# Two linear-attention blocks on one core: the column sums of pk finished on VectorE through DRAM instead of on TensorE, with two rows of M loaded earlier

## The chip, the core and the metric

One of the eight cores of a Trainium2 chip runs the whole program. The metric is the time of one execution on the device in microseconds (us). Three runs of the kernel before took 577.52, 580.03 and 580.3 us, median 580.03.

The engines are named as in the profile: PE is TensorE (matmuls), DVE is VectorE, ACT is ScalarE, POOL is GpSimd, SP is SyncE, which here only issues DMAs. Each engine runs its own list of instructions in program order, and waits where a semaphore says that its operand is not there or its buffer not free.

## What is computed

Two independent blocks A and B, each with x of 2048 x 640, 32 heads of 20 columns, and fp32 throughout. The outputs of the two are laid side by side.

```python
qkv = (x @ wqkv).reshape(B, S, 3, H, Dh)...
phi = lambda t: jnp.where(t > 0, t + 1, jnp.exp(t)) + 1e-6
pq, pk = phi(q), phi(k)
kv  = jnp.einsum("bhsd,bhse->bhde", pk, v)
z   = jnp.einsum("bhsd->bhd", pk)
num = jnp.einsum("bhqd,bhde->bhqe", pq, kv)
den = jnp.einsum("bhqd,bhd->bhq", pq, z)[..., None] + 1e-6
return (num / den) ... @ wo
```

z, the column sums of pk over the 2048 rows, is what this change is about.

## The kernel before

Every fp32 product is made of three matmuls on halves: ACT rounds an operand to a high part (names that end in h), DVE subtracts it and keeps the low part (names that end in l: pkl, xnl, wql, xql, dsl), and PE adds high by high, high by low and low by high in PSUM (L209 to L211, and L349 for the products that save a multiplication by sums of quarters of the operands).

**The first phase** runs over the 32 tiles of 128 rows of x, block 0 (A) first and then block 1. Steps are PE's work, and jobs are the work of the other engines and the DMAs. Each step has a position; each job has a place beside a step. The tables MOVED (steps) and SHIFT (jobs) move them by hand-set numbers, and perform() (L397) issues all in the sorted order. That order, and nothing else, sets each engine's list.

- The steps ("p", i, n) are the products pk = x Wk of a pair of tiles (kprod, L494). ACT copies the results out of PSUM, DVE adds them (L356), ACT makes exp and relu, DVE mixes the two to ek (L564), POOL accumulates ek into a 128x640 tile in DRAM with an adding DMA (phi_z, L572, tile zd), ACT rounds to pkh (L576) and DVE makes pkl (L580).
- The steps ("G", i, s) and ("H", i, s, h) are the sums of x transposed times pk over four tiles (gsum, psg). DVE adds them to gacc (gacc_add, L650).
- After block 0 come kv = Wv x gacc, masked to the heads (kvmm, L776), and M = kv Wo (mev), stored to DRAM (md). Later rows of M are read back (load_w with "m", L233, tile wst), and DVE makes sums of them (form_sums1 and form_sums2, L854 to L862), which the products of the second phase need.
- Block 0's z: when all 16 tiles are in zd, SP reads the tile back (load_z, L731, tile zs), and five fp32 products with a column of ones (zmm, L733 to L737) make z in PSUM, five columns of 128. Each shows as two matmuls of 128x1 in the trace. z_out (L742 to L744) adds the epsilon on DVE and makes the sum of z.

**The second phase** has eight q groups u of 512 rows, four for each block. Its slots are written by hand: ("q", u, c, k) is product k of column block c of q = x Wq (psq), ("o", u, s) is stage s of the output product. at(slot, f, ...) hangs other work onto a slot, and run(slot) issues it there. In a group, ACT and DVE make phi of q (L944 to L946), DVE accumulates the denominators with z (qacc, L956), PE adds them over the heads (denmm, L967), DVE takes the reciprocal (L972), divides, and makes sums and splits of the quotient, and PE multiplies by the forms of M (outmm).

Block 1's kv and M are made inside the first q groups (kv_step, m_step). Block 1's zs is read back by SP just behind the loads of the first q group's x (xqs, xql), once the last accumulation into zd has landed. z_step, hung on ("q", 0, 1, 0), makes the ten matmuls and z_out. Block 1's z is first needed in group u = 4.

Between the phases stands a stretch in which DVE adds the last gsums (gacc of group 7), splits Wq (wql) and x (xql), while PE runs the last G and H steps, turns a part of gacc (T), and then starts ("q", 0, 0, 0). SP's loads of x for it (xqs, L277) wait for buffers that these splits free.

Of the kernel before, what the change touches and what calls it, by code (L numbers as in the profile page):

```python
# [14 lines left out]
H = 32  # L15
# [4 lines left out]
    ('c0', 10): 1.48, ('c0', 14): 1.59, ('c0', 3): 0.53, ('c0', 7): 1.14, ('c0', 8): 0.83, ('c0', 9): 2.95, ('c2',  # L20
    14): 0.45, ('c2', 6): 0.21, ('c2', 8): 1.01, ('c2', 9): 0.64, ('c4', 15): 0.47, ('c5', 10): 0.45, ('c5', 8):
    1.14, ('constants',): 2.19, ('exp', 0): 1.25, ('exp', 10): 0.43, ('exp', 11): 0.65, ('exp', 12): 2.78, ('exp',
    14): 0.41, ('exp', 15): 0.95, ('exp', 16): 0.91, ('exp', 2): 1.22, ('exp', 20): 0.06, ('exp', 22): 2.23, ('exp',
    23): 0.68, ('exp', 24): 0.16, ('exp', 25): 1.33, ('exp', 26): -0.21, ('exp', 28): 1.07, ('exp', 3): 4.78,
# [15 lines left out]
    2.01, ('gacc', 3, 3): 2.94, ('gacc', 4, 4): 0.78, ('gacc', 4, 5): 1.22, ('gacc', 7, 1): 0.62, ('gacc', 7, 2):  # L40
    1.9, ('kt', 1): 1.13, ('kvh', 4): 1.1, ('kvl', 0): 1.72, ('kvl', 1): 3.28, ('kvl', 2): 0.84, ('kvl', 3): 2.08,
    ('kvl', 4): 2.85, ('kvl', 5): 0.1, ('ld', 'k', 1, 1): -0.66, ('ld', 'k', 1, 2): 1.83, ('ld', 'k', 1, 3): -3.06,
    ('ld', 'k', 1, 4): 1.19, ('ld', 'm', 0, 0): 1.3, ('ld', 'm', 0, 2): 1.3, ('ld', 'm', 0, 4): 0.78, ('mix', 0):
# [1527 lines left out]
```

## Time and profile before

| | us |
|---|---|
| median of three runs | 580.03 |
| lowest, highest run | 577.52, 580.3 |
| the profiled execution | 580.78 |
| its span, first to last instruction | 579.0 |
| PE busy | 568.6 |
| DVE, ACT, POOL busy | 436.1, 335.8, 84.8 |
| mean granted PE clock | 0.996 |

How to read the rows that are quoted below. A row of the timeline begins with its start and its length in us, then the engine, the line, the operation, the tiles written and read (out<-in), the shape, and how many instructions were joined; in brackets stands the idle time before it and what ended it. PE's matmuls overlap, so the distance from one start to the next is what each one costs, not its length. A row of a group by line gives the total, the mean in ns, and the idle time before. A row of the waits gives total us, the number of waits, and the longest. In a table of windows the five pairs are the busy us (and instructions) of PE, PE's weight loads, DVE, ACT and POOL, then come the granted clock, the DMA share and GB/s.

### The profile page before, as it was taken

Reading aid. Unit: us, or ns where it says so; the run is one execution under the profiler, and the core shown is the slowest. Engines: PE = TensorE matmul, PEld = TensorE weight load, DVE = VectorE, ACT = ScalarE, POOL = GpSimd, SP = SyncE. Lnnn points to the kernel's source line nnn. Section 1 sums busy time; section 2 is a strip of 40 time slices with the busy share of each in tenths; the row PEclk is TensorE's granted clock in tenths of the full one; section 3 lists DMA queues with packets and bytes.
Section 4 is the critical chain, followed back from the end, with each engine's and each line's share of the span. In section 5 each row is a group of like instructions: output and inputs, shape, how many; then the busy total and the mean of one; then the engine's idle time right before and its main releaser. Section 6 shows DMA issues by size and latency. Waiting matters only on the chain.

```text
span 579.0 us, 9075 instructions
## 1 busy us (share of the span) xinstructions
PE 568.6 (98%) x3263; PEld 516.7 (89%) x3263; DVE 436.1 (75%) x724; ACT 335.8 (58%) x625; POOL 84.8 (15%) x141
## 2 busy tenths in 40 slices
PE   8999999999999999999989999999999999999997
PEld 6989999888999998978878889898998989898997
DVE  5889599877484868779735698977799776767792
ACT  5864567663674874746634865755657364545541
POOL 0111132411011211223200101311011200001010
PEclk9999999999999999999999999999999999999999
DMA  7968789899986877978989985764263994122022
GB/s 253 245 157 210 191 227 328 230 337 353 315 220 158 210 174 167 324 221 239 292 246 311 294 282 176 258 202 150 75 248 133 374 380 144 70 65 92 0 92 91
DMA packets 70260, 123.54 MB, mean 213 GB/s; under 512 B 7560, under 2 KB 32520, under 8 KB 70216
## 3 DMA queue, kind: packets, MB, share of 16 engines
q1 hardware_dynamic: 57912, 83.25, 44.9%
q0 software_dynamic: 12160, 39.66, 24.7%
q8 instruction: 25, 0.41, 0.3%
q14 instruction: 19, 0.16, 0.1%
q10 hardware_dynamic: 144, 0.07, 0.0%
HBM read 73.60 MB, written 49.35 MB: 212 GB/s over the span
## 4 chain that ended last, share of the span: by engine, by line
PE 86%; DMA 8%; DVE 2%; issue 2%; ACT 1%; SPq 1%; POOL 0%; DVEq 0%; POOLq 0%
PE pa L349 19%; PE pe L349 10%; PE psq L209 8%; PE psq L211 8%; PE psq L210 8%; PE psg L210 6%; PE psg L211 6%; PE psg L209 6%; PE psb L349 6%; PE psk L605 4%; DMA zd<-ek 3%; DMA wst<-md 2%; PE pskv L776 2%; DMA xn<-in_B_x 1%; DMA x<-in_A_xt_tiles 1%
## 5 line engine op out<-in xcount | busy, mean ns | idle before, releaser
L209 PE MATMUL psq<-xqh,wqh 128*128 128x512 f32 x200 | 79.2, 396 | 0.0
L210 PE MATMUL psq<-xql,wqh 128*128 128x512 f32 x200 | 78.5, 393 | 0.0
L211 PE MATMUL psq<-xqh,wql 128*128 128x512 f32 x200 | 78.4, 392 | 0.0
L210 PE MATMUL psg<-pkl,xnh 128*128 128x512 f32 x160 | 62.9, 393 | 1.4 <-DVE pkl L580 1.4
L209 PE MATMUL psg<-pkh,xnh 128*128 128x512 f32 x160 | 62.9, 393 | 0.0
L211 PE MATMUL psg<-pkh,xnl 128*128 128x512 f32 x160 | 62.5, 391 | 0.3 <-DVE xnl L199 0.3
L353 ACT ACTIVATE o<-pa 128x320 f32<-128x320 f32 x64 | 27.9, 438 | 45.2 <-PE pa L349 45.1
L946 DVE SCALAR_TENSOR_TENSOR pq<-eq,rq 128x512 f32<-128x512 f32 x40 | 27.6, 690 | 28.3 <-ACT rq L945 28.3
L572 POOL DMA_DIRECT2D zd<-ek x30 | 26.4, 881 | 133.1 <-DVE ek L564 65.2
L211 PEld LDWEIGHTS psq<-xqh,wql 128*128 128x128 f32 x200 | 38.0, 190 | 8.0
L210 PEld LDWEIGHTS psq<-xql,wqh 128*128 128x128 f32 x200 | 38.0, 190 | 7.4
L209 PEld LDWEIGHTS psq<-xqh,wqh 128*128 128x128 f32 x200 | 38.0, 190 | 7.3
L944 ACT ACTIVATE eq<-psq 128x512 f32<-128x512 f32 x40 | 23.8, 596 | 34.3 <-PE psq L211 32.0
L353 ACT ACTIVATE ko<-pa 128x320 f32<-128x320 f32 x52 | 22.4, 433 | 33.3 <-PE pa L349 33.0
L210 PEld LDWEIGHTS psg<-pkl,xnh 128*128 128x128 f32 x160 | 30.1, 188 | 7.7 <-DVE pkl L580 2.6
L576 ACT ACTIVATE pkh<-ek,epst 128x640 fp32r<-128x640 f32 x32 | 26.3, 826 | 17.9 <-DVE ek L564 17.9
L211 PEld LDWEIGHTS psg<-pkh,xnl 128*128 128x128 f32 x160 | 30.0, 188 | 7.3 <-DVE xnl L199 0.9
L209 PEld LDWEIGHTS psg<-pkh,xnh 128*128 128x128 f32 x160 | 30.1, 188 | 5.1
L650 DVE TENSOR_TENSOR gacc<-psg,gacc 128x512 f32<-128x512 f32 (+2 forms) x42 | 26.4, 628 | 6.9 <-PE psg L211 6.7
L202 ACT ACTIVATE dah<-pq 128x1024 fp32r<-128x1024 f32 (+5 forms) x27 | 18.2, 708 | 20.4 <-DVE pq L978 20.4
L580 DVE SCALAR_TENSOR_TENSOR pkl<-ek,pkh 128x640 fp32r<-128x640 f32 x32 | 26.1, 819 | 4.9 <-ACT pkh L576 4.9
L440 ACT ACTIVATE ksh<-sx 128x512 fp32r<-128x512 f32 x26 | 16.3, 627 | 23.1 <-DVE sx L458 22.9
(208 smaller groups left out, 1697.6 us busy)
## 6 DMA issues: line engine op xcount, KB each, us to landing
zd<-ek POOLq DMA_DIRECT2D x32, 320.0 KB, 5.1
out<-o POOLq DMA_DIRECT2D x28, 320.0 KB, 3.6
xql<-xd SPq DMA_DIRECT2D x24, 256.0 KB, 4.3
xn<-in_A_x SPq DMA_DIRECT2D x16, 320.0 KB, 4.8
...
xqs<-in_A_xt SPq DMA_DIRECT2D x20, 256.0 KB, 5.9
xqs<-in_B_xt SPq DMA_DIRECT2D x20, 256.0 KB, 4.4
```

The costliest lines, as they stand in the source:

```text
L209: nc.tensor.matmul(o, whi, xhi, start=first, stop=False)
L210: nc.tensor.matmul(o, whi, xlo, start=False, stop=False)
L211: nc.tensor.matmul(o, wlo, xhi, start=False, stop=last)
L349: nc.tensor.matmul(o, x, y, start=start and m == r == 0, stop=m == len(terms) - 1 and r == 2, skip_group_check=True)
L353: nc.scalar.activation(x, y, AF.Copy)
L572: nc.gpsimd.dma_start(zacc[b], e, accum_op=OP.add)
L576: nc.scalar.activation(pk[n][0], ek[n], AF.Identity, bias=epst)
L580: nc.vector.scalar_tensor_tensor(lo, ek[n], EPS, f32(hi), op0=OP.add, op1=OP.subtract)
L605: nc.tensor.matmul(kps["c", n][h], plain_x(n, c)[i], plain_w(c)[j][:, h * HF:(h + 1) * HF], start=(c == 0 and i == j == 0), stop=(c == NC ...
L650: nc.vector.tensor_tensor(o, x, o, op=OP.add)
L944: nc.scalar.activation(e, ps, AF.Exp)
L946: nc.vector.scalar_tensor_tensor(pq[u][:, c, :], e, 1.0, r, op0=OP.min, op1=OP.add)
```

## The change

The column of ones and zmm go. Each block's z is finished in these steps instead: read zd back (load_z); transpose it in 32x32 blocks on DVE and sum each block's 32 columns, 640 values a partition to 20 (z_turn); store 128x20 to DRAM (z_store); read it back as 32x4x5 in four DMAs so that the parts of one column lie on one partition (z_back, pieces of five floats); add the four parts, the epsilon and the total on DVE (z_out, now four operations).

Block 0's steps are jobs of the first phase: load_z beside ("p", 11, 0), z_turn beside ("p", 12, 3), z_store at ("g", 5, 3), z_back beside ("p", 14, 1), z_out at the first sum of group 7. Block 1's go into the second q group (u = 1) and the third.

The loads of rows 1 and 3 of M (form_jobs "m") move from ("p", 13, 4) to ("g", 5, 6). A new table AT moves six calls of the second phase by one or two slots. Of SHIFT and MOVED most entries are new: many steps and jobs change place with a neighbour. store_m takes one more argument, which it does not use.

```diff
-    ('c0', 10): 1.48, ('c0', 14): 1.59, ('c0', 3): 0.53, ('c0', 7): 1.14, ('c0', 8): 0.83, ('c0', 9): 2.95, ('c2',
+    ('c0', 10): 1.48, ('c0', 11): 0.04, ('c0', 12): 1.46, ('c0', 14): 3.31, ('c0', 3): 1.17, ('c0', 6): 0.26, ('c0',
...
+AT = {
+    ('denmm', 1): 2, ('kv_step', 1, 4): 2, ('m_step', 1, 3): 1, ('recip', 1, 0): 1, ('split_acc', 1): 1, ('z_turn',
+    1): 2,
+}
...
     def at(slot, f, *a):
+        slot = line[line.index(slot) + AT.get((f.__name__,) + a, 0)]
         todo.setdefault(slot, []).append((f, a))
...
-    ones = base.tile([P, 1], F32)
...
     def load_z(b):
-        wst["z", b] = base.tile([P, D], F32, name="zs", tag=f"wo{'hl'[b]}", bufs=2)
-        nc.sync.dma_start(wst["z", b], zacc[b])
-
-    def zmm(b):
-        x = wst["z", b]
-        zps[b] = bank("psz", "small")
-        for c in range(NC):
-            nc.tensor.matmul(zps[b][:, c:c + 1], x[:, c * P:(c + 1) * P], ones, start=True, stop=True)
+        zt[b] = base.tile([P, D], F32, name="zs", tag=f"wo{'hl'[b]}", bufs=2)
+        nc.sync.dma_start(zt[b], zacc[b])
+
+    def z_turn(b):
+        t = base.tile([P, D], F32, name="zt", tag=f"wo{'lh'[b]}", bufs=2)
+        nc.vector.transpose(t, zt[b])
+        zt[b] = base.tile([P, 2, 4 * NC], F32, name="zr", tag="kvt", bufs=3)
+        nc.vector.tensor_reduce(zt[b][:, 0].rearrange("p (j c) -> p c j", j=4),
+                                t.rearrange("p (c j a) -> p c j a", c=NC, j=4), axis=mybir.AxisListType.X, op=OP.add)
+
+    def z_store(b):
+        zr[b] = dram.tile([4, 32, 4 * NC], F32, name=f"zr{b}")
+        nc.sync.dma_start(zr[b].rearrange("i b c -> (i b) c"), zt[b][:, 0])
+
+    def z_back(b):
+        for j in range(4):
+            nc.sync.dma_start(zt[b][32 * j:32 * (j + 1), 1].rearrange("b (i c) -> b i c", i=4),
+                              zr[b][:, :, NC * j:NC * (j + 1)].rearrange("i b c -> b i c"))
 
     def z_out(b):
...
-        nc.vector.tensor_scalar(z, zps[b][:, :NC], S * EPS, None, op0=OP.add)
+        nc.vector.tensor_reduce(z, zt[b][:, 1].rearrange("p (i c) -> p c i", i=4),
+                                axis=mybir.AxisListType.X, op=OP.add)
+        nc.vector.tensor_scalar(z, z, S * EPS, None, op0=OP.add)
...
-            step(("z",), zmm, 0, after=[("zl",)])
...
-    form_jobs("m", 0, ([("g", 5, 5), ("p", 13, 4), ("g", 5, 5), ("p", 13, 4), ("g", 6, 1)],
+    form_jobs("m", 0, ([("g", 5, 5), ("g", 5, 6), ("g", 5, 5), ("g", 5, 6), ("g", 6, 1)],
...
-    job(("zl",), ("p", 9, 2), load_z, 0, after=[("zs", n) for n in range(NT)])
-    job(("zo",), ("z",), z_out, 0, after=[("z",)])
-    job(("zl1",), ("g", LG, 7), load_z, 1, after=[("zs", n) for n in range(NT, NN)])
+    job(("zl",), ("p", 11, 0), load_z, 0, after=[("zs", n) for n in range(NT)])
+    job(("zt",), ("p", 12, 3), z_turn, 0, after=[("zl",)])
+    job(("zw",), ("g", 5, 3), z_store, 0, after=[("zt",)])
+    job(("zb",), ("p", 14, 1), z_back, 0, after=[("zw",)])
+    job(("zo",), ("g", LG, 0), z_out, 0, after=[("zb",)])
...
-    at(("q", 0, 1, 0), z_step, 1)
+    at(("q", 1, 2, 3), load_z, 1)
+    at(("q", 1, 3, 3), z_turn, 1)
+    at(("q", 1, 4, 2), z_store, 1)
+    at(("q", 2, 0, 0), z_back, 1)
+    at(("q", 2, 2, 0), z_out, 1)
```

Three places of the lists, before and after. Line numbers of the changed kernel are higher by 21 to 37 (L210 becomes L231, L580 becomes L605).

**TensorE in the second column block of the first q group.** psq is the q product, psz the column sums of block 1, pskv the kv product of block 1. Before:

```order
L210 MATMUL psq<-xql,wqh 128x512
L211 MATMUL psq<-xqh,wql 128x512
L737 MATMUL psz<-ones,zs 128x1 x5
L776 MATMUL pskv<-gacc,wv 120x120 x5
L209 MATMUL psq<-xqh,wqh 128x512
L210 MATMUL psq<-xql,wqh 128x512
```

After:

```order
L231 MATMUL psq<-xql,wqh 128x512
L232 MATMUL psq<-xqh,wql 128x512
L809 MATMUL pskv<-gacc,wv 120x120 x5
L230 MATMUL psq<-xqh,wqh 128x512
L231 MATMUL psq<-xql,wqh 128x512
```

The five column-sum products are gone, and the kv product follows the q product.

**VectorE in the first phase, around the pkl of tiles 26 and 27** (ek and ko belong to phi, wst is a row of M, t_ the sums made of it). Before:

```order
L564 SCALAR_TENSOR_TENSOR ek<-ek,ko 128x640
L356 TENSOR_TENSOR ko<-pe,ko 128x320
L854 TENSOR_TENSOR t_3029<-wst 128x320
L855 TENSOR_TENSOR wst<-wst 128x320
L580 SCALAR_TENSOR_TENSOR pkl<-ek,pkh 128x640 x2
L861 TENSOR_TENSOR t_3029<-wst 128x320
L862 TENSOR_TENSOR t_3060<-wst,t_3029 128x320
```

After:

```order
L220 TENSOR_TENSOR fsl<-t_2822,fsh 128x320
L887 TENSOR_TENSOR t_3011<-wst 128x320
L888 TENSOR_TENSOR wst<-wst 128x320
L381 TENSOR_TENSOR ko<-pe,ko 128x320
L589 SCALAR_TENSOR_TENSOR ek<-ek,ko 128x640
L894 TENSOR_TENSOR t_3011<-wst 128x320
L895 TENSOR_TENSOR t_3029<-wst,t_3011 128x320
L605 SCALAR_TENSOR_TENSOR pkl<-ek,pkh 128x640 x2
```

The four operations on wst and t_ now all stand ahead of the pkl, and the last ek behind the first two of them.

**SyncE's queue in the same stretch** holds the loads of M (wst<-md), those of x (xn, xt) and the stores of x's halves (xd). Before:

```order
L233 DMA wst<-md_2200 128x640 x2
L417 DMA xn<-in_B_x 128x640 x2
L270 DMA xd_2452<-kal 128x3x128
L272 DMA xd_2452<-kal 128x128
L417 DMA xt<-in_B_xt_tiles 128x640
L270 DMA xd_2686<-kal 128x3x128
L417 DMA xn<-in_B_x 128x640
L272 DMA xd_2686<-kal 128x128
L417 DMA xn<-in_B_x 128x640 x3
L417 DMA xt<-in_B_xt_tiles 128x640
L233 DMA wst<-md_2200 128x640 x3
```

After:

```order
L260 DMA wst<-md_2186 128x640 x3
L299 DMA xd_2406<-kal 128x128
L297 DMA xd_2406<-kal 128x3x128
L260 DMA wst<-md_2186 128x640
L442 DMA xn<-in_B_x 128x640 x2
L297 DMA xd_2656<-kal 128x3x128
L442 DMA xn<-in_B_x 128x640
L442 DMA xt<-in_B_xt_tiles 128x640
L442 DMA xn<-in_B_x 128x640
L442 DMA xt<-in_B_xt_tiles 128x640
L442 DMA xn<-in_B_x 128x640 x2
```

Rows 1 and 3 of M (in the second load row before) stood behind eight loads of x; now they stand ahead of them.

**VectorE between the phases** (gacc<-psg adds the last gsums, wql and xql split Wq and x, z and zs are block 0's z_out). Before:

```order
L580 SCALAR_TENSOR_TENSOR pkl<-ek,pkh 128x640
L650 TENSOR_TENSOR gacc<-psg,gacc 128x3x128
L199 TENSOR_TENSOR wql<-wst,wqh 128x640
L650 TENSOR_TENSOR gacc<-psg,gacc 128x512
L199 TENSOR_TENSOR wql<-wst,wqh 128x640
L650 TENSOR_TENSOR gacc<-psg,gacc 128x2x128
L199 TENSOR_TENSOR wql<-wst,wqh 128x640
L650 TENSOR_TENSOR gacc<-psg,gacc 128x512
L199 TENSOR_TENSOR wql<-wst,wqh 128x640
L199 TENSOR_TENSOR xql<-xqs,xqh 128x2x128
L650 TENSOR_TENSOR gacc<-psg,gacc 128x512
L199 TENSOR_TENSOR xql<-xqs,xqh 128x2x128
```

After:

```order
L605 SCALAR_TENSOR_TENSOR pkl<-ek,pkh 128x640
L220 TENSOR_TENSOR wql<-wst,wqh 128x640 x2
L777 TENSOR_REDUCE z<-zr 128x5
L779 TENSOR_SCALAR z<-z 128x5
L780 TENSOR_REDUCE zs<-z 128x1
L781 TENSOR_SCALAR zs<-zs 128x1
L675 TENSOR_TENSOR gacc<-psg,gacc 128x3x128
L675 TENSOR_TENSOR gacc<-psg,gacc 128x512 x3
L675 TENSOR_TENSOR gacc<-psg,gacc 128x2x128
L220 TENSOR_TENSOR xql<-xqs,xqh 128x2x128
L220 TENSOR_TENSOR wql<-wst,wqh 128x640
L220 TENSOR_TENSOR xql<-xqs,xqh 128x2x128
```

z_out of block 0 and a second wql now stand ahead of the first sum, the five sums follow each other, and the other splits come after them.

More of the change, by code (lines that the diff above doesn't have):

```diff
@@ L19 @@
 SHIFT = {
-    ('c0', 10): 1.48, ('c0', 14): 1.59, ('c0', 3): 0.53, ('c0', 7): 1.14, ('c0', 8): 0.83, ('c0', 9): 2.95, ('c2',
[L21 to L24, printed above, removed]
[6 rows of a table removed]
@@ L31 @@
-    ('fdl', 'm', 0, 1): 0.25, ('fdl', 'm', 0, 3): 0.24, ('fdl', 'm', 0, 4): -0.49, ('fdl', 'm', 0, 6): 0.19, ('fdl',
[8 rows of a table removed]
[L40 to L43, printed above, removed]
@@ L92 @@
-    ('wol', 5): 0.05, ('wq', 0): 0.26, ('wq', 3): 0.21, ('wq', 4): 0.82, ('wqh', 0): -0.07, ('wqh', 1): -0.75,
-    ('wqh', 2): -1.14, ('wqh', 3): -1.22, ('wqh', 4): -3.33, ('wql', 0): -0.07, ('wql', 1): 1.4, ('wql', 2): -0.14,
[28 rows of a table removed]
-    -1.62, ('xq', 4): -2.08, ('xqh', 0): -0.26, ('xqh', 1): 0.24, ('xqh', 2): 0.5, ('xqh', 3): -1.19, ('xqh', 4):
-    -3.5, ('xql', 0): 0.23, ('xql', 1): -0.7, ('xraw', 0): -4.48, ('xraw', 1): 0.25, ('xraw', 2): -0.5, ('xraw', 3):
[3 rows of a table removed]
[4 rows of a table added]
+    10): 0.04, ('exp', 11): 0.73, ('exp', 12): 2.92, ('exp', 13): 3.23, ('exp', 14): 0.41, ('exp', 15): 0.95,
@@ new lines @@
+    ('exp', 16): 0.91, ('exp', 17): 0.07, ('exp', 18): -0.02, ('exp', 2): 0.61, ('exp', 20): -0.96, ('exp', 22):
+    1.7, ('exp', 25): 0.96, ('exp', 28): 1.07, ('exp', 3): 4.78, ('exp', 4): 0.2, ('exp', 5): 3.19, ('exp', 6):
[3 rows of a table added]
+    ('fdh', 'k', 1, 6): 0.01, ('fdh', 'k', 1, 8): 4.09, ('fdh', 'm', 0, 0): 1.04, ('fdh', 'm', 0, 1): 1.71, ('fdh',
[3 rows of a table added]
+    ('fdl', 'm', 0, 0): -0.93, ('fdl', 'm', 0, 1): -0.43, ('fdl', 'm', 0, 2): 1.2, ('fdl', 'm', 0, 3): 0.76, ('fdl',
[8 rows of a table added]
+    ('gacc', 0, 0): 0.46, ('gacc', 0, 1): 3.2, ('gacc', 0, 3): 0.36, ('gacc', 0, 5): 1.67, ('gacc', 0, 6): 1.73,
@@ new lines @@
+    ('gacc', 1, 1): 0.04, ('gacc', 1, 3): 0.64, ('gacc', 1, 5): 1.74, ('gacc', 1, 6): 1.99, ('gacc', 2, 1): 2.89,
+    ('gacc', 2, 3): 0.28, ('gacc', 3, 0): 0.42, ('gacc', 3, 1): 2.82, ('gacc', 3, 2): 2.99, ('gacc', 3, 3): 3.83,
+    ('gacc', 3, 5): 2.14, ('gacc', 3, 6): 1.96, ('gacc', 4, 0): 0.75, ('gacc', 4, 4): 2.17, ('gacc', 4, 5): 5.31,
+    ('gacc', 5, 0): 0.6, ('gacc', 5, 3): 1.28, ('gacc', 5, 5): 0.51, ('gacc', 5, 6): 1.36, ('gacc', 6, 2): 0.82,
+    ('gacc', 6, 4): 0.59, ('gacc', 7, 0): 0.31, ('gacc', 7, 1): 0.04, ('gacc', 7, 2): 2.56, ('gacc', 7, 4): 0.07,
@@ new lines @@
+    ('gacc', 7, 5): 0.78, ('gacc', 7, 6): 2.69, ('iota', 0): 1.42, ('kt', 0): 0.53, ('kt', 1): 1.13, ('kt', 5):
+    3.35, ('kvh', 0): 1.2, ('kvh', 1): 5.05, ('kvh', 4): 1.1, ('kvl', 1): 2.02, ('kvl', 2): 0.84, ('kvl', 3): 2.08,
+    ('kvl', 5): 1.36, ('ld', 'k', 1, 0): 1.32, ('ld', 'k', 1, 1): -0.06, ('ld', 'k', 1, 2): -2.17, ('ld', 'k', 1,
+    3): -3.61, ('ld', 'k', 1, 4): -1.63, ('ld', 'm', 0, 0): 1.22, ('ld', 'm', 0, 1): 1.16, ('ld', 'm', 0, 2): 1.48,
+    ('ld', 'm', 0, 3): -0.03, ('mc', 4, 1): 0.69, ('mix', 0): -0.53, ('mix', 10): 0.15, ('mix', 11): 0.24, ('mix',
@@ new lines @@
+    12): 0.49, ('mix', 13): 7.61, ('mix', 14): 4.05, ('mix', 15): 0.17, ('mix', 19): 1.66, ('mix', 20): 0.31,
+    ('mix', 23): 0.53, ('mix', 24): -0.1, ('mix', 26): 0.21, ('mix', 29): 2.36, ('mix', 3): -0.55, ('mix', 30): 0.8,
+    ('mix', 4): 3.06, ('mix', 5): 7.59, ('mix', 7): 1.86, ('mix', 8): 3.89, ('mix', 9): 1.16, ('ms', 0): -0.08,
[23 rows of a table added]
+    10): 1.37, ('relu', 11): 0.09, ('relu', 13): 1.06, ('relu', 14): 1.59, ('relu', 17): 1.12, ('relu', 2): 0.27,
+    ('relu', 21): 4.79, ('relu', 25): 2.55, ('relu', 28): 1.48, ('relu', 29): 0.1, ('relu', 30): 3.49, ('relu', 5):
[15 rows of a table added]
@@ new lines @@
+    -0.23, ('turn', 0, 0): 0.01, ('turn', 1, 0): 1.68, ('turn', 1, 1): 7.33, ('unit', 1): -2.53, ('v', 0): -0.59,
[6 rows of a table added]
+    1.07, ('woh', 1): -0.68, ('woh', 4): -0.51, ('wol', 0): 0.5, ('wol', 3): 0.03, ('wol', 4): 0.03, ('wq', 0):
+    -1.7, ('wq', 1): -0.97, ('wq', 3): -3.63, ('wq', 4): 9.05, ('wqh', 0): -2.09, ('wqh', 1): -2.1, ('wqh', 2):
+    -0.81, ('wqh', 4): -1.58, ('wql', 0): 0.07, ('wql', 1): -0.07, ('wql', 2): 7.63, ('wql', 3): 2.02, ('wql', 4):
[23 rows of a table added]
+    0): 1.47, ('xq', 2): -6.23, ('xq', 3): -7.53, ('xqh', 0): 0.62, ('xqh', 1): 0.38, ('xqh', 2): 0.96, ('xqh', 3):
@@ L127 @@
+    -1.51, ('xqh', 4): -0.13, ('xql', 0): 0.88, ('xql', 1): 0.44, ('xraw', 0): -2.59, ('xraw', 1): -1.73, ('xraw',
[4 rows of a table added]
 }
 MOVED = {
[7 rows of a table removed]
[13 rows of a table added]
+}
+AT = {
+    ('denmm', 1): 2, ('kv_step', 1, 4): 2, ('m_step', 1, 3): 1, ('recip', 1, 0): 1, ('split_acc', 1): 1, ('z_turn',
+    1): 2,
 }
@@ L214, in tile_linear_attn_pair @@
     todo = {}
+    line = []
+    for u in range(NU + 1):
+        line += [("q", u, c, k) for c in range(NC) for k in range(NC)] * (u < NU)
+        line += [("o", u - 1, s) for s in range(14)] * (u > 0)
     def at(slot, f, *a):
+        slot = line[line.index(slot) + AT.get((f.__name__,) + a, 0)]
         todo.setdefault(slot, []).append((f, a))
@@ L308, in constants @@
     def constants():
-        nc.vector.memset(ones, 1.0)
         ij = base.tile([P, P], I32, name="ij", tag="kvt", bufs=3)
@@ L724, in group_places @@
                 place["g", i, s] = share(i, 0.1 * (s + 1) if s >= halves else 0.15 + 0.05 * (s + 1))
[L726 removed]
+    zz, zt, zr, md, wvt, wot, kvt, kvp, mps = {}, {}, {}, {}, {}, {}, {}, {}, {}
     written = []
     def load_z(b):
[L730 to L737 removed]
+        zt[b] = base.tile([P, D], F32, name="zs", tag=f"wo{'hl'[b]}", bufs=2)
[13 more added lines that the diff above has]
+                              zr[b][:, :, NC * j:NC * (j + 1)].rearrange("i b c -> b i c"))
     def z_out(b):
@@ L745, in z_out @@
         zz[b] = z, s
-    def z_step(b):
-        zmm(b)
-        z_out(b)
     def load_v(b, g):
@@ L841, in m_step, with store_m @@
             m_out(b, g, h)
-    def store_m(eng):
+    def store_m(eng, g):
         eng.dma_start(*written.pop(0))
@@ L1401, in tile_linear_attn_pair @@
             job(("mc", g, k), ("m", g), m_out, 0, g, k, after=[("m", g)] + [("mc", g, 0)] * k)
-        job(("ms", g), place["m", g] + 1, store_m, nc.gpsimd, after=[("mc", g, 1)])
-    form_jobs("m", 0, ([("g", 5, 5), ("p", 13, 4), ("g", 5, 5), ("p", 13, 4), ("g", 6, 1)],
+        job(("ms", g), place["m", g] + 1, store_m, nc.gpsimd, g, after=[("mc", g, 1)])
+    form_jobs("m", 0, ([("g", 5, 5), ("g", 5, 6), ("g", 5, 5), ("g", 5, 6), ("g", 6, 1)],
                        [("g", 5, 8), ("p", 14, 4)], [("g", 5, 9), h(6, 1)], ("g", 6, 4),
@@ L1438, in tile_linear_attn_pair @@
         at((("q", 0, 2, 4), ("q", 0, 3, 4), ("q", 1, 0, 1), ("q", 1, 0, 3), ("q", 1, 1, 4), ("q", 1, 2, 4))[g],
-           store_m, nc.gpsimd)
+           store_m, nc.gpsimd, g)
     def forms(w, b, places):
```

6 lines of the change are left out of this document (removed), and 196 rows, old and new, of tables (MOVED, SHIFT).

## The prediction

> **What bounds the kernel now.** I read the busy times first, then the page's list of what TensorE waited for.
>
> ```profile
> PE 568.6 (98%) x3263; PEld 516.7 (89%) x3263; DVE 436.1 (75%) x724; ACT 335.8 (58%) x625; POOL 84.8 (15%) x141
> ...
> PE psz L737 <- DMA zs<-zd: 1.7, 1, 1.7
> PE psg L210 <- DVE pkl L580: 1.4, 2, 1.2
> ...
> PE psg L211 <- DVE pkl L580: 0.2, 1, 0.2
> PE pe L349 <- DVE o L356: 0.2, 1, 0.2
> ```
>
> PE is busy in 568.6 of 579.0 us. So a change can only gain by taking work off PE, by removing one of its few waits, or by removing time at a low clock. The longest wait, 1.7 us, stands before the column sums (psz, L737). The timeline of PE there, and the table of windows that covers the end of it (its columns after the five engines are the granted clock, the DMA share and GB/s):
>
> ```profile
> 296.92 0.39 PE L210 MATMUL psq<-xql,wqh 128*128 128x512 f32 x1
> 297.15 0.40 PE L211 MATMUL psq<-xqh,wql 128*128 128x512 f32 x1
> 299.25 1.28 PE L737 MATMUL psz<-ones,zs 128*128 128x1 f32 x10 [1.71 <-DMA zs<-zd]
> 300.39 1.41 PE L776 MATMUL pskv<-gacc,wv 128*120 128x120 f32 x10
> 301.46 0.78 PE L209 MATMUL psq<-xqh,wqh 128*128 128x512 f32 x1
> 302.04 0.63 PE L210 MATMUL psq<-xql,wqh 128*128 128x512 f32 x1
> ...
> 304.94 0.39 PE L211 MATMUL psq<-xqh,wql 128*128 128x512 f32 x1
> 301.41:304.83 3.42, 3.42 (x11) 2.74 (x10) 1.09 (x3) 1.04 (x2) 0.00 (x0) 0.50 1.06 248
> ```
>
> Here three losses follow each other: 1.71 us of idling, 1.14 us of zmm (299.25 to 300.39), and 3.42 us with the clock granted at 0.50. The chain of waits says why the sums came late:
>
> ```profile
> 288.94 7.21 DMA zd<-ek
> 296.27 2.94 DMA zs<-zd
> ```
>
> The last accumulation into DRAM (zd) took 7.21 us, its reading back 2.94, and PE stood behind both.
>
> **What the change removes.** Block 0 has the same ten matmuls without a wait:
>
> ```profile
> 165.29 1.21 PE L737 MATMUL psz<-ones,zs 128*128 128x1 f32 x10
> 166.36 0.48 PE L209 MATMUL psg<-pkh,xnh 128*128 128x512 f32 x1
> ```
>
> The next matmul starts 1.07 us later. Both zmm leave PE for good: 1.07 + 1.14 = **2.21 us**. The wait on zs goes too: **1.71**. Nothing else is late there: the next step on PE, kv_step(1, 1), needs a weight load that the changed order issues earlier than before.
>
> The half clock: from 301.46 to 304.94 eight matmuls start. At full speed their starts are 0.23 us apart (296.92 and 297.15), so 8 x 0.23 = 1.84 instead of 3.48: **1.64 us**, if the gap ahead of them causes it. I take it so, because it is the only halved stretch between start and end and it follows directly on the longest stretch without wide matmuls (297.4 to 301.4).
>
> [...]
>
> The second wait sits at 249. On DVE (first three rows) and PE (the others):
>
> ```profile
> 248.80 0.49 DVE L854 TENSOR_TENSOR t<-wst 128x320 f32<-128x320 f32 x1 [2.22 <-DMA wst<-md]
> 249.32 0.49 DVE L855 TENSOR_TENSOR wst<-wst 128x320 f32<-128x320 f32 x1
> 249.74 1.55 DVE L580 SCALAR_TENSOR_TENSOR pkl<-ek,pkh 128x640 fp32r<-128x640 f32 x2
> ...
> 249.05 0.40 PE L209 MATMUL psg<-pkh,xnh 128*128 128x512 f32 x1
> 250.60 0.50 PE L210 MATMUL psg<-pkl,xnh 128*128 128x512 f32 x1 [1.16 <-DVE pkl L580]
> ```
>
> DVE idles 2.22 us for a row of M that was loaded behind loads of x, does two form sums, and only then makes the pkl that PE wants. In the changed order rows 1 and 3 of M are issued ahead of eight loads of x instead of behind them, so all four form sums stand ahead of that pkl with their data long there. The start distance on PE is 1.55 against 0.23, so 1.3 is to be had. The pkl now follows its own chain (ek, pkh on ACT) and ends at about 249.2 by my count, just when PE wants it. I take **1.2**.
>
> The short waits. A wait of 0.2 in the list costs more than its idle time, since the next start is late by the pipeline as well:
>
> ```profile
> 357.44 0.46 PE L349 MATMUL pe<-f,dah 128*128 128x320 f32 x2
> 357.73 0.31 PE L349 MATMUL pe<-f,dal 128*128 128x320 f32 x1
> 358.21 0.42 PE L349 MATMUL pe<-fh,dsh 128*128 128x320 f32 x1 [0.17 <-DVE o L356]
> ```
>
> Starts 0.48 apart where 0.15 is usual (two in the 0.29 from 357.44): 0.33 for a listed 0.17. Three such waits are touched: this one (a reciprocal on DVE stood ahead of o and is moved behind it), the second pkl wait of L210 (1.4 - 1.16 = 0.24 listed) and that of L211 (0.2), whose pkl are made earlier or used later. Twice the listed 0.6 is 1.2; I take **1.05**.
>
> Sum of the gains: 2.21 + 1.71 + 1.64 + 1.2 + 1.05 = **7.8 us**.
>
> **What it adds.** The trace of before has neither a transpose nor a reduction of 128x640 on DVE. The nearest rows are the cheapest and the dearest rate of DVE:
>
> ```profile
> L972 DVE RECIPROCAL rd<-psd 128x256 f32<-128x256 f32 x16 | 27.8, 1745 | 0.9 <-PE psd L967 0.9
> L580 DVE SCALAR_TENSOR_TENSOR pkl<-ek,pkh 128x640 fp32r<-128x640 f32 x32 | 26.1, 819 | 4.9 <-ACT pkh L576 4.9
> 208.00:215.20 7.20, 6.98 (x41) 6.11 (x39) 4.42 (x7) 5.90 (x10) 1.75 (x2) 1.00 0.60 125
> 346.67 1.22 DVE L199 TENSOR_TENSOR dsl<-sr,dsh 128x1024 fp32r<-128x1024 f32 x1
> 351.28 0.31 PE L349 MATMUL pa<-fh,dsh 128*128 128x320 f32 x1
> ```
>
> By L580 each costs 0.82, so a z_turn 1.6 us; by the reciprocal's rate (1.745 x 640/256 = 4.36) 8.7. All plain 128x640 rows of DVE lie at 0.82, so I take 1.6. [...]
>
> Block 0's turn stands at about 207. DVE is busy 4.42 of the 7.20 us after 208 (the fourth pair in the window row), so 2.8 us of slack hide it before the next pkl that PE waits for (the 0.24 of L210) is due. Block 1's turn stands in the second q group, where DVE runs behind PE, between two splits, ahead of the dsl that ends at 347.89; PE first uses that half of the sums at 351.28. Cover: 3.4 us. Both at nothing; without the cover it would be 1.6 each.
>
> The stores and loads of z (128x20, and 512 pieces of 20 bytes) run on SP's queue. Each has at least 10 us between issue and use; the smallest transfers of before landed in 2.9 to 5 us. Nothing.
>
> The place that does cost is the entry into the q phase. The last sums of block 1 on DVE, their first user on PE, and the loads of x that follow:
>
> ```profile
> 281.88 0.83 DVE L580 SCALAR_TENSOR_TENSOR pkl<-ek,pkh 128x640 fp32r<-128x640 f32 x1 [0.90 <-ACT pkh L576]
> L650 DVE TENSOR_TENSOR gacc<-psg,gacc 128x512 f32<-128x512 f32 (+2 forms) x42 | 26.4, 628 | 6.9 <-PE psg L211 6.7
> L199 DVE TENSOR_TENSOR wql<-wst,wqh 128x640 fp32r<-128x640 f32 x10 | 8.1, 811 | 0.3 <-ACT wqh L238 0.3
> L743 DVE TENSOR_REDUCE zs<-z x2: 157/158/158, 169.0 to 300.8; 128x1 f32<-128x5 f32 x2
> 286.17 0.39 PE L209 MATMUL psg<-pkh,xnh 128*128 128x512 f32 x1
> 288.36 0.42 DVE L199 TENSOR_TENSOR xql<-xqs,xqh 128x256 fp32r<-128x256 f32 x1
> 286.08 1.39 SPq L277 DMA_DIRECT2D xqs<-in_A_xt  x2
> xqs<-in_A_xt SPq DMA_DIRECT2D x20, 256.0 KB, 5.9
> 292.14 1.16 ACT L290 ACTIVATE xqh<-xqs 128x512 fp32r<-128x512 f32 x2 [0.39 <-DMA xqs<-in_A_xt]
> 293.55 0.39 PE L209 MATMUL psq<-xqh,wqh 128*128 128x512 f32 x1
> ```
>
> After the pkl (end 282.7) DVE now has two wql (2 x 0.8), the four small operations of z_out (4 x 0.16), and only then the sums gacc 5, 0, 2, 1, 6. That puts the second of them at 282.7 + 1.6 + 0.7 + 0.5 + 0.6 = 286.1. PE, freed of the L211 wait just ahead (0.4 by the doubling above), wants that bank at about 286.17 - 0.4 = 285.8: a wait of 0.3, or twice that if the fifth sum, which the turn of gacc on PE needs, is late too; I take **0.5**. Further, the last load of x (issued by 286.08 + 1.39 = 287.5 before) now waits for the xql that ends about 288.1. In before that load landed 4.7 us after its issue, at 292.1, and ACT made two xqh by 293.3, used at 293.55. Now: 288.1 + 4.7 to 5.9, plus 1.2 on ACT, is 294.0 to 295.2 against a use at 293.55 + 0.4 = 294.0: 0 to 1.2. I take **0.35**. What the refitted tables do elsewhere (over a hundred steps and jobs change place by one or two neighbours) I could follow only at the tightest places; for it I set down **0.4**, between nothing and rival (c).
>
> The sum: 7.8 - 0.5 - 0.35 - 0.4 = 6.55. The profiled execution took 580.78 (span 579.0), which gives 574.2; it lies 0.75 above the median of 580.03, which would give 573.5. I take **574.0**, nearer to the execution that the rows come from.
>
> **The rivals.** A measurement of this kernel can tell about 0.5% from no change, so "same" is 577.1 to 582.9.
>
> (a) A new wait takes the place of the old one at the q entry: the late load of x lands at 295.2 or later, PE waits 1.2 to 1.5 us amid narrow kv matmuls, and the clock halves again (1.64). Loss about 3.2 on the forecast: 577.2. For: ACT idled 0.39 us for this load in before already. Against: it is issued only 0.6 us later.
>
> (b) The halved stretch does not come from the gap and stays: 574.0 + 1.64 = 575.6. For: the gap of 1.16 us at 249 halved nothing, so a gap alone does not do it. Against: its place. [...]
>
> (c) The new order of the neighbours brings as many short waits as it takes: the 1.2 of pkl and the 1.05 come back elsewhere, and one more of 1.2 with them: 574.0 + 3.5 = 577.5. For: at 249 and 357 (rows above) PE waited for work that DVE merely had in an unlucky order. Against: I found no such place in the order.
>
> (d) Slower: DVE's transpose and reduction run at the reciprocal's rate. A turn of 8.7 us exceeds the cover by 8.7 - 2.8 = 5.9 in block 0 and 8.7 - 3.4 = 5.3 in block 1, both on PE: 574.0 + 11.2 = 585.2. It passes 582.9 once a turn takes more than 7.6 us (2 x 7.6 - 6.2 = 9.0). For: only that no row shows them. Against: the other 128x640 rows are all near 0.82.
>
> **How the numbers follow.** Forecast (571.2 to 576.5) 0.58; (a) 0.13; (b) 0.10; (c) 0.12; (d) 0.07. (a) and (c) lie just past 577.1; three tenths of their 0.25 count as faster: 0.58 + 0.10 + 0.07 = 0.75. The rest of them is same: 0.18; slower is (d): 0.07. Low end: all gains, no cost, from the median: 580.03 - 7.8 = 572.2, and 1 us for the spread of the runs (577.52 to 580.3): 571.2. High end: (a) or (c) with 1 us more: 578.7.
>
> **What would show it.** Right: no psz rows; the granted clock at 1.00 from start to end; PE's list without zs, with pkl at 249 gone or under 0.3; transpose and reduction near 0.8 us each; short waits at the q entry on gacc, on xqh or both. Wrong: a wait above 1 us at the first psq matmuls (a); a 0.50 stretch without a long gap ahead of it (b); new pkl, xnl or ko waits that sum to 3 us (c); a turn above 3 us with PE waiting on dsl (d).

## The result and the profile after

The changed kernel took 573.01 us (median of 7 runs, 571.96 to 575.27) against 577.61 (7 runs, 577.41 to 580.3): a ratio of 0.9917, 95% interval 0.9892 to 0.9943. Measured again beside the kernel before (a_repeat below), it was 573.51 against 579.45, ratio 0.9898 (0.9871 to 0.9925). The ratios come from the single runs and are not the quotients of the medians; the two differ by up to 0.2%. The forecast was 574.0, a gain of 6.0 to 6.55; the two measurements give 4.6 and 5.9. The profiled executions lie further apart: spans 579.0 and 571.0.

PE's busy time and its whole list of waits, after:

```profile
PE 564.1 (99%) x3243; PEld 514.1 (90%) x3243; DVE 438.2 (77%) x729; ACT 334.5 (59%) x625; POOL 84.5 (15%) x141
...
PE psq L230 <- ACT xqh L317: 1.2, 1, 1.2
PE psi L1124 <- DVE idle L1121: 1.0, 1, 1.0
PE pa L374 <- ACT ko L378: 0.5, 1, 0.5
PE psk L630 <- DVE wl L220: 0.4, 1, 0.4
PE pa L374 <- ACT mev L378: 0.2, 1, 0.2
```

No wait on zs, none on pkl, none on o; and 20 instructions fewer on PE. Two waits are new: xqh, 1.2 us, now the longest, and mev, 0.2 us. The timeline of PE at the place of the old column sums, and the table of windows over the q entry (the granted clock is the last column but two):

```profile
294.33 0.39 PE L232 MATMUL psq<-xqh,wql 128*128 128x512 f32 x1
294.56 1.21 PE L809 MATMUL pskv<-gacc,wv 128*120 128x120 f32 x10
...
285.00:290.00 5.00, 4.42 (x20) 3.28 (x18) 2.62 (x4) 0.59 (x2) 0.00 (x0) 1.00 0.93 287
290.00:295.00 5.00, 4.38 (x27) 3.85 (x28) 1.00 (x4) 2.80 (x7) 0.00 (x0) 1.00 0.80 240
```

The kv product follows the q product at the usual 0.23 us, at full clock. The two windows hold 1.2 us in which PE is not busy, and that is the xqh wait. How it comes about, on PE, DVE, SP and ACT in turn:

```profile
289.02 0.40 PE L232 MATMUL psq<-xqh,wql 128*128 128x512 f32 x1
290.62 0.50 PE L230 MATMUL psq<-xqh,wqh 128*128 128x512 f32 x1 [1.20 <-ACT xqh L317]
...
280.46 2.71 DVE L675 TENSOR_TENSOR gacc<-psg,gacc 128x384 f32<-128x384 f32 x5
283.08 0.41 DVE L220 TENSOR_TENSOR xql<-xqs,xqh 128x256 fp32r<-128x256 f32 x1
283.53 0.33 SPq L304 DMA_DIRECT2D xqs<-in_A_xt  x1
289.41 1.15 ACT L317 ACTIVATE xqh<-xqs 128x512 fp32r<-128x512 f32 x2 [7.09 <-DMA xqs<-in_A_xt]
```

Five sums of gacc run without a pause on DVE (280.46 to 283.17), then xql frees the buffer, SP issues the last load of x at 283.53, it lands 5.9 us later, and only then does ACT make the two xqh.

The two new operations of DVE, by line:

```profile
L760 DVE STREAM_TRANSPOSE zt<-zs 128x640 f32<-128x640 f32 x2 | 1.7, 837 | 0.0
L762 DVE TENSOR_REDUCE zr<-zt 128x20 f32<-128x640 f32 x2 | 1.6, 821 | 0.1
```

A turn costs 1.66 us, as the 128x640 rows had it.

### The profile page after: what moved, and what is told of

Same layout as the page of the kernel before. It is cut to its first block, busy times and chain, and to the rows that moved or that the text cites. A ratio compares the mean times of both kernels' runs of the same rounds, so it can differ in the third digit from the quotient of the medians.

```text
span 571.0 us, 9065 instructions
## 1 busy us (share of the span) xinstructions
PE 564.1 (99%) x3243; PEld 514.1 (90%) x3243; DVE 438.2 (77%) x729; ACT 334.5 (59%) x625; POOL 84.5 (15%) x141
## 4 chain that ended last, share of the span: by engine, by line
PE 87%; DMA 6%; ACT 3%; DVE 2%; issue 1%; SPq 0%; POOL 0%; DVEq 0%; ACTq 0%; POOLq 0%
PE pa L374 21%; PE pe L374 10%; PE psq L230 8%; PE psq L232 8%; PE psq L231 8%; PE psb L374 6%; PE psg L232 6%; PE psg L231 6%; PE psg L230 6%; PE psk L630 4%; PE pskv L809 2%; DMA md<-mev 2%; DMA zd<-ek 1%; DMA wst<-md 1%; DMA xqs<-in_A_xt 1%
## 5 line engine op out<-in xcount | busy, mean ns | idle before, releaser
L231 PE MATMUL psq<-xql,wqh 128*128 128x512 f32 x200 | 77.9, 389 | 0.0
L231 PE MATMUL psg<-pkl,xnh 128*128 128x512 f32 x160 | 62.7, 392 | 0.0
L231 PEld LDWEIGHTS psq<-xql,wqh 128*128 128x128 f32 x200 | 37.6, 188 | 7.2
L231 PEld LDWEIGHTS psg<-pkl,xnh 128*128 128x128 f32 x160 | 30.0, 188 | 5.7 <-DVE pkl L605 0.3
L220 DVE TENSOR_TENSOR xnl<-xn,xnh 128x640 fp32r<-128x640 f32 x32 | 25.9, 820 | 6.9 <-ACT xnh L509 6.8
L605 DVE SCALAR_TENSOR_TENSOR pkl<-ek,pkh 128x640 fp32r<-128x640 f32 x32 | 25.9, 821 | 6.5 <-ACT pkh L601 6.3
```

Of the source, the lines that this page charges most:

```text
L220: nc.vector.tensor_tensor(lo, src, f32(hi), op=OP.subtract)
L231: nc.tensor.matmul(o, whi, xlo, start=False, stop=False)
L605: nc.vector.scalar_tensor_tensor(lo, ek[n], EPS, f32(hi), op0=OP.add, op1=OP.subtract)
```

## The experiments

All medians stand beside runs of the kernel before on the same chip. Where less than one per cent matters the rows of the profiles are read first, since single times of one kernel scatter by 2 to 8 us.

**The kernel before once more (b_repeat).**

> The kernel before, unchanged. Its runs so far lie at 577.4 to 577.9 and at 580.0 to 580.8. Theory A: the difference is two things that fall out differently from run to run, the half-clock stretch behind the wait on zs (1.6 us) and PE's wait at the start on the first pieces of x (1.3 us). Then the wait on zs (1.7 us) is in this profile again, near 297 us, and the time follows the other two: about 577.5 with neither, 580.8 with both. Rival B: the half clock always follows the wait, and the runs differ elsewhere; then a 0.50 stretch of 3.4 us stands behind the wait in this profile too, whatever the time.

Measured: 579.79 (before beside it 579.53), span 578.3. On PE, and the windows around the wait and behind it:

```profile
298.58 1.27 PE L737 MATMUL psz<-ones,zs 128*128 128x1 f32 x10 [2.08 <-DMA zs<-zd]
...
296.10:300.14 4.04, 1.96 (x16) 1.56 (x15) 0.90 (x3) 1.64 (x3) 0.00 (x0) 1.00 0.91 270
300.15:303.56 3.41, 3.41 (x14) 2.99 (x13) 0.94 (x5) 1.04 (x2) 0.00 (x0) 0.50 1.03 277
```

The wait is there again, 2.08 us, and the clock halves again for 3.41 us. The 1.3 us at the start (PE on the first pieces of x) is not. The changed kernel's profile does not have it either, and the next PE row that both share starts 1.0 us earlier there (9.08 against 10.08). ACT waited 0.78 us for a piece of x there in the profile of before, and in that of the change not at all. So it was one execution's luck with a transfer, and about 1.0 of the 8.0 us between the two profiles has nothing to do with the change. The mean clock was recorded for 73 executions of this kernel, ten of this run and 63 beside the experiments. In 29 it is 0.999 to 1.000, mean time 578.0; in 30 it is 0.996 or 0.997 (one halved stretch of 3.41 in 577), mean 579.8; in 14 it is 0.993 or 0.994 (two; the profile of a_oldrows below has 6.82 us at half clock and 0.994), mean 581.5. So an execution takes about 1.8 us more for each stretch, and before had 0.79 of them on average (58 in 73). The changed kernel's 11 executions with a recorded clock all have 0.999 or 1.000. Theory A holds in its main point: both profiles have the wait, and the half clock comes in only a part of the executions. Against rival B speaks the next run, whose profile has a wait of 1.95 us at a clock of 0.999.

**Only the matmuls of block 1's sums later (b_late).**

```diff
-    at(("q", 0, 1, 0), z_step, 1)
+    at(("q", 0, 3, 0), z_step, 1)
```

> The kernel before with one edit: the ten column-sum matmuls of block 1 stand two column blocks later in the first q group, when their data has landed. zmm stays on PE (1.1 us), only the wait goes. Theory A: the wait of 1.7 us goes and with it any half clock, so 1.7 to 3.4 us less than before, 0.994 to 0.997 of it, with no row psz <- zs in PE's list of waits. Rival C (the gain needs PE to be rid of zmm, or the wait moves to what stands behind it on SP's queue, the weight loads of kv): under 1 us gained, and PE waits for a weight load near 297 instead.

Measured: ratio 1.0006 (0.9983 to 1.0029), 578.71. A miss. PE, DVE, ACT and SP:

```profile
303.86 1.31 PE L776 MATMUL pskv<-gacc,wv 128*120 128x120 f32 x10 [1.95 <-DVE kvt L783]
302.79 0.82 DVE L199 TENSOR_TENSOR wol<-wo,woh 120x640 fp32r<-120x640 f32 x1 [3.95 <-ACT woh L805]
302.02 0.74 ACT L805 ACTIVATE woh<-wo 120x640 fp32r<-120x640 f32 x1 [3.50 <-DMA wo<-in_B_wo]
...
287.28 3.26 SPq L754 DMA_DIRECT2D wv<-in_B_wv  x3
294.51 0.33 SPq L731 DMA_DIRECT2D zs<-zd  x1
294.93 1.33 SPq L754 DMA_DIRECT2D wv<-in_B_wv  x3
296.35 2.88 SPq L766 DMA_DIRECT2D wo<-in_B_wo  x6
```

The wait moved to a later kv step and kept its size. load_z(1) still stands in SP's queue, between two halves of the loads of wv, until the last accumulation has landed: SP is held from 290.54 to 294.51, 4.0 us. The loads of wo stand behind it; kvt stands behind wol on DVE, and PE behind kvt. Rival C had the queue right and named the wrong load.

**Load and matmuls both in the second q group, still on PE (b_free).**

```diff
-    job(("zl1",), ("g", LG, 7), load_z, 1, after=[("zs", n) for n in range(NT, NN)])
...
-    at(("q", 0, 1, 0), z_step, 1)
+    at(("q", 1, 2, 3), load_z, 1)
+    at(("q", 1, 4, 0), z_step, 1)
```

> The kernel before with block 1's column sums still on PE, but both the load of zs and the matmuls moved to the second q group, so that SP's queue is not held up in front of the loads of wo. With only the matmuls moved, PE waited 1.95 us for kvt behind a late wo instead. Theory A (what cost the time was the load of zs that blocks SP's queue, not zmm): neither wait is left between 290 and 310, the clock stays at 1.00, and the span is 1.7 to 3.4 us below that of before, 575 to 576.5. Rival G (the loads that now run together delay xqs or wv): a new wait above 0.7 us on xqh or pskv between 290 and 310, span 577 or more.

Measured: ratio 0.9945 (0.9915 to 0.9976), 575.56 against 579.45, span 573.2, clock 0.999 or 1.000 in all five runs. The top of PE's list, and SP's loads of wo:

```profile
PE psi L1091 <- DVE idle L1088: 1.0, 1, 1.0
PE pa L349 <- ACT ko L353: 0.5, 1, 0.5
...
293.78 2.87 SPq L766 DMA_DIRECT2D wo<-in_B_wo  x6
```

Nothing waits between 290 and 310 any more; wo is issued 2.6 us sooner than in b_late (296.35). Theory A, and the gain of 3.9 us is more than the 1.7 to 3.4 expected. About two thirds of the change's gain on the same chip (3.9 of 5.9) is had by moving block 1's load and matmuls, without VectorE. What is left to the changed kernel (573.51) is 2.05 us. That is near the 2.21 of zmm, but it is no measurement of zmm: the rows of M, the refitted tables and the new wait on xqh lie in the same difference.

**Only the rows of M earlier (b_rows).**

```diff
-    form_jobs("m", 0, ([("g", 5, 5), ("p", 13, 4), ("g", 5, 5), ("p", 13, 4), ("g", 6, 1)],
+    form_jobs("m", 0, ([("g", 5, 5), ("g", 5, 6), ("g", 5, 5), ("g", 5, 6), ("g", 6, 1)],
```

> The kernel before with one edit: the loads of rows 1 and 3 of M at the earlier place. Theory A: the pkl wait near 249 us (1.16 listed, 1.3 to 1.4 in start distances) goes and nothing takes its place: 1.2 to 1.4 us less, 0.998 of before. Rival D: the x loads that now stand behind them come later and PE waits for xnl or ko in the same stage: no change, with a new wait of 0.5 to 1.5 us between 235 and 270.

Measured: ratio 0.9978 (0.9952 to 1.0004), 578.34: the time does not tell the two apart. The profile shows both: the pkl wait at 249 is gone, and a wait of 0.7 on ko near 236 has come (in the second line of its list; the other 0.5 was there before).

```profile
PE psz L737 <- DMA zs<-zd: 1.3, 1, 1.3
PE pa L349 <- ACT ko L353: 1.2, 2, 0.7
```

And the wait that was to be saved varies from one execution to the next: 1.16 at this place in the profile of before, 0.33 in b_repeat, none in b_late. DVE's idling there for the row of M varies with it: 2.22, 1.39 and 1.15 us.

**Only the column sums on VectorE (b_zonly).** The functions and slots of the change (with the places of its z jobs), otherwise the old tables and the old loads of M.

> The kernel before with the column sums of both blocks on VectorE as in the change, but with the old tables of places and the old loads of M. Theory A: 2.2 us of zmm, 1.7 us of waiting, and the half clock where it had come: 3.9 to 5.5 less than before, about 0.991 to 0.993, so nearly all that the change brings; the pkl wait near 249 stays at 1.2. Rival E: without the refitted places the turn of block 0 or z_out delays DVE at the tight places, and PE waits 1 to 3 us more near 207, 215 or 285: 1 to 3 less than before.

Measured: ratio 0.9997 (0.9964 to 1.0031), 580.36, span 581.5. Nothing gained, and theory A falls. Rival E had the loss, but not the place where most of it arose. PE, DVE and SP near 250, and the window behind the wait:

```profile
255.69 0.79 PE L210 MATMUL psg<-pkl,xnh 128*128 128x512 f32 x1 [4.43 <-DVE pkl L580]
253.88 0.49 DVE L862 TENSOR_TENSOR t<-wst 128x320 f32<-128x320 f32 x1 [5.29 <-DMA wst<-md]
...
243.83 1.89 SPq L746 DMA_DIRECT2D zr<-zr  x4
245.76 1.61 SPq L233 DMA_DIRECT2D wst<-md  x3
...
255.21:258.62 3.41, 2.93 (x7) 2.35 (x8) 3.18 (x6) 1.10 (x3) 0.85 (x2) 0.50 0.69 176
```

z_back's four issues take 1.89 us on SP, ahead of the rows of M. DVE waits 5.29 us for those rows with pkl behind them, PE 4.43 for pkl, and the clock halves. This profile is of the slowest of the ten executions (583.31); four others at full clock took 575.7 to 577.4, so this wait, too, is not the same in all.

**Column sums and rows of M, old tables (b_zrows).** b_zonly with the edit of b_rows.

> The kernel before with both visible parts of the change, the column sums on VectorE and the early loads of rows 1 and 3 of M, but with the old tables of places and no shifts of the second phase's calls. The run with the column sums alone gained nothing: four loads of z on SP's queue, 1.9 us of issuing, pushed the rows of M back, and PE waited 4.4 us for pkl, with the clock halved behind it. Theory A (the parts need each other): the pkl wait near 250 falls under 0.5 and the half clock goes, while the waits of that run at 209 to 217 (2.1 us in start distances, the turn of block 0 waiting for its load) and before the denominators near 352 (psd <- ac, 1.3 us) stay: span 575 to 576, against 581.5 with the column sums alone and 571.0 of the change. Rival F (the refitted tables do nothing): span 571 to 572.5.

Measured: ratio 0.9962 (0.9938 to 0.9986), 576.89, span 574.4, clock 0.999 or more in all five. The wait at 250 is gone: theory A, with a span a little below the 575 to 576 expected. Left in its list, among others:

```profile
PE psd L974 <- ACT ac L202: 0.6, 1, 0.6
PE psg L209 <- ACT pkh L576: 0.4, 1, 0.4
PE psg L210 <- DVE pkl L580: 0.4, 1, 0.4
```

The two visible parts need each other; the refitted tables are worth another 3.4 us (576.89 to 573.51; spans 574.4 to 571.3). On the same chip b_free, which keeps zmm on PE, took 575.56. So with the old tables the way over VectorE shows no advantage over moving zmm, and whether the refit on top of b_free would have given as much was not run.

**Rows of M back at the old place in the changed kernel (a_oldrows).** The line of b_rows, reversed.

> The changed kernel with rows 1 and 3 of M loaded at their old place, behind eight loads of x and now also behind the four loads that bring block 0's z back (1.7 us of issuing on SP). Theory A (the early rows are what pays for z's four loads): DVE waits for wst near 242 to 250 with all four form sums ahead of pkl, PE waits for pkl 3 to 6 us there, the clock halves behind it in some executions, and the span is 575 to 579. Rival F: the refitted places around it give enough slack, PE waits under 1 us there, span 571 to 572.5.

Measured: ratio 1.0038 (1.0014 to 1.0062), 581.43, span 578.5: 0.4% slower than before. Rival F falls. DVE, PE, and the window:

```profile
248.69 0.49 DVE L887 TENSOR_TENSOR t<-wst 128x320 f32<-128x320 f32 x1 [6.59 <-DMA wst<-md]
250.16 0.64 PE L374 MATMUL pe<-wfh,ksh 128*128 128x320 f32 x1 [4.14 <-DVE ko L381]
...
249.10:255.92 6.82, 5.76 (x17) 5.09 (x18) 5.34 (x10) 3.78 (x6) 1.46 (x3) 0.50 0.49 101
```

One line of the change is worth 7 us of span (578.5 against 571.3 of a_repeat, on another chip) once z_back stands in the queue. PE waits for ko, not pkl, and the clock is halved for 6.82 us, twice the 3.41 of b_repeat; eight of nine executions have 0.994.

**Three turns for block 1 (a_turn3).** `for _ in range(1 + 2 * b)` around the transpose and the reduction.

> The changed kernel with block 1's transpose and reduction made three times (the same result), 3.3 us more on DVE between the two splits of the second q group. It measures the cover that the prediction put at 3.4 us before the turn (so 1.7 left after it). By the trace of the change the dsl behind it ends at 341.2 and PE first needs it at 343.5 (2.3 left); the ac of the denominators ends at 344.95 and PE needs it at 345.8 (0.9 left). Theory A: PE waits about 1.0 on dsl and 1.4 on ac, 2.0 to 2.4 in all, span 573 to 573.7. Rival I (DVE has slack enough there, the turn is free whatever its size): no new wait, span 571 to 571.5. Rival J (DVE is the bound there): the full 3.3, span 574.3 or more.

Measured: 575.95, ratio 0.9953 (0.993 to 0.9977), span 573.6. PE:

```profile
344.19 0.41 PE L374 MATMUL pa<-fh,dsl 128*128 128x320 f32 x1 [1.08 <-DVE dsl L220]
347.96 0.50 PE L1002 MATMUL psd<-ac,same 128*128 128x512 f32 x1 [0.92 <-DVE ac L220]
```

Theory A: both covers end where the trace of the change had them, dsl by 1.08 (1.0 expected), ac by 0.92 and two tenths more (1.4 expected).

**The q entry (a_xql, a_repeat, a_swap, a_both).** a_repeat is the changed kernel. The edits of a_xql and of a_swap; a_both has all three lines:

```diff
-    ('xqh', 1): 0.38,  ('xql', 1): 0.44,
+    ('xqh', 1): -0.7,  ('xql', 1): -0.9,
...
-    ('xqh', 2): 0.96,
+    ('xqh', 2): -0.3,
```

> The changed kernel, unchanged, as the neighbour of the others on this chip. Theory A: the wait on xqh of 1.2 us at the third product of the q phase is set by the order (the load is issued when xql is done) and by a transfer of 4.5 to 6 us, so it is there again, between 0 and 1.5 us, and no 0.50 stretch stands between start and end. Rival B: the clock halves behind that wait in some executions, which gives spans near 572.5 to 573.5, as two of the seven runs had.

> The changed kernel with one edit: the first xql split (of x's block 1) stands ahead of the last two sums of block 1 on DVE instead of behind them. It frees the buffer for which SP holds the last load of x. Theory A: that load is issued 0.8 to 0.9 us sooner (283.5 before), PE's wait for xqh at the third product of the q phase falls from 1.2 to 0.3 or 0.4, and the span by 0.8 (570.2). Rival H: the sum of gacc for the turn is 0.3 to 0.4 late now, and PE waits there instead, or the transfer takes the longer for sharing: span 570.8 to 571.5, with a wait on gacc near 283.

> The changed kernel with one edit: ACT rounds x's block 2 before block 3 for the first q group. Block 2 landed about 4 us earlier, PE needs it first, and ACT has it behind block 3, whose load is issued last. Theory A (the new wait of 1.2 to 1.4 us is this order on ACT): PE's wait for xqh falls to 0 to 0.4, since block 3 is needed only 0.7 us after block 2; span about 570, 1.0 to 1.3 us below the change beside it. Rival H: what ACT does behind it, the turn of gacc and the last xqh, is the next to be late; PE waits 0.6 us or more at pskv or at the fourth or fifth product, and the span falls by less than 0.6.

> The changed kernel with both edits at the q entry: ACT rounds block 2 before block 3, and DVE splits xql ahead of the last two sums, so that the last load is issued 0.8 us sooner. Theory A: no wait for xqh above 0.1, span 569.7 to 570.2, the shortest of all; against the order on ACT alone 0 to 0.3 us less. Rival H: the sum for the turn of gacc becomes late (0.1 to 0.4 us at pst), and nothing is gained over the order on ACT alone.

Measured: a_repeat 573.51, span 571.3, wait 1.4, clock 1.000 in all four executions, so theory A there and not rival B; a_xql 573.47, span 572.4; on a second chip a_swap 574.28, span 571.2, and a_both 572.47, span 570.4. a_xql's list has the xqh wait down to 0.5 (0.3 or 0.4 expected), but two others up (in a_repeat ko had 0.5 and mev was not listed), so its span does not show the gain:

```profile
PE pa L374 <- ACT ko L378: 1.3, 2, 0.8
...
PE psq L230 <- ACT xqh L317: 0.5, 1, 0.5
PE pa L374 <- ACT mev L378: 0.5, 1, 0.5
```

a_swap missed. ACT and PE:

```profile
285.45 0.63 ACT L317 ACTIVATE xqh<-xqs 128x512 fp32r<-128x512 f32 x1 [2.79 <-DMA xqs<-in_A_xt]
290.55 0.63 ACT L317 ACTIVATE xqh<-xqs 128x512 fp32r<-128x512 f32 x1 [4.47 <-DMA xqs<-in_A_xt]
291.23 0.50 PE L230 MATMUL psq<-xqh,wqh 128*128 128x512 f32 x1 [1.41 <-ACT xqh L317]
```

Block 2 is ready 4 us sooner than in the change, and PE waits just as long one product later, for block 3. So the landing of the last load sets the wait, not ACT's order alone. But the edit also moved that load: SP issues it at 286.10 here, behind ACT's first of these two xqh (which ends at 286.08), and not at 283.53 behind xql. So this run does not test ACT's order with the load held in place. With both edits the load is issued at 282.90, ACT has block 3 here, and nothing waits for xqh:

```profile
288.86 0.63 ACT L317 ACTIVATE xqh<-xqs 128x512 fp32r<-128x512 f32 x1 [1.93 <-DMA xqs<-in_A_xt]
```

a_both has the shortest span of all, a little above the 569.7 to 570.2 expected, and a ratio of 0.9892 (0.9861 to 0.9923) to before. That it beats the changed kernel (0.9917 and 0.9898) these intervals do not show.

## Why the prediction was right

**zmm, 2.21: right as time on PE.** The rows are gone. What this alone is worth to the whole no run shows: b_free, which keeps zmm, is 2.05 us slower than the change, but differs from it in more than zmm.

**The wait on zs, 1.71: right in the sum, incomplete in its reason.** I wrote that nothing else is late there because the weight load of kv_step comes earlier. b_late shows a second wait, of 1.95, at a later kv step, on wo. It goes only because the load of zs leaves SP's queue at that place, which the change also does.

**The half clock, 1.64: right in that it goes when the waits go; the size holds for one execution.** None of the 11 executions of the change and of the five of b_free has a halved stretch. One costs about 1.8 us, but 29 of 73 executions of before have none. The profiled execution had one, and I took the sum from it; on the average of 0.79 stretches it is 1.4, and against an execution without any it is 0. The five runs of before at 577.4 to 577.9 lie where the executions at full clock lie (mean 578.0); their clock was not recorded. That would account for the difference between the 6.0 forecast and the 4.6 measured; it was not shown.

**pkl at 249, 1.2: mis-sized.** It is gone as said. But the term came from the worst of the executions seen: b_repeat has 0.33 there, b_late nothing. And the reason was only half: the rows of M had to move because z_back's four issues stand ahead of them. I priced SP's queue at nothing by the time between issue and use, and counted neither the 1.89 us of issuing nor who stands behind. Without the early rows the change loses 7 us (a_oldrows). That would have been a rival with a slower end, and I had not seen it.

**The short waits, 1.05: right in place.** None of the three is in the list of after. In a_repeat a wait of 0.24 on pkl stands at another place, and what the three cost together was not measured apart.

**The turn: right in its price** (1.66, taken 1.6; rival (d) needed 7.6), **wrong in its cover.** I named the dsl, 3.4 us. The tighter one is ac of the denominators: with the old slots, PE waits there (b_zrows, 0.6 and 0.2), and in the change, where denmm stands two slots later, 0.9 us is left.

**The q entry, 0.5 + 0.35: right in place, wrong in parts.** No wait on gacc came (PE's product into that bank starts at 281.80 without a gap). The xqh wait was 1.2 to 1.4, at and above the upper end of the 0 to 1.2 I gave. This is rival (a)'s wait in size, and a wait above 1 us there was a sign that I had named for being wrong. It came without the half clock, so the price of 3.2 was not paid.

**Elsewhere, 0.4: about right.** One small wait came into the list (mev, 0.2), where (c) had feared 3.5.

**What was luck.** Two gains came from one execution that had them at or near their largest (half clock, pkl), and the costs at the q entry were put too low in one part and too high in the other. An estimate with the averages of the profiles instead (half clock 1.4, pkl about 0.5 in place of 1.2, xqh about 1.5 between starts in place of 0.35, no gacc, 0.3 for mev) gives about 5 us, between the two measured gains of 4.6 and 5.9. The high end of the range was added wrongly: rival (c)'s 577.5 with 1 us more is 578.5, not 578.7; nothing hangs on it.

PE's gaps ahead of a halved stretch were 1.71 us in the profile of before and 2.08 in b_repeat, where PE was busy for 1.96 of the 4.04 us ahead of it. Rival (b) falls, since the stretch did not stay. What stays open is whether the gap alone did it: in both profiles zmm and a kv product or a part of it, all narrow matmuls, stand between the gap and the stretch. From the end of the last wide matmul to the stretch passed 3.9 and 3.65 us there; from one wide matmul to the next it was 3.0 us in b_late and 3.5 in b_rows, whose profiles are at full clock.
